# Query scores to a second bank, their casts four steps later, and one batch assigned three steps later

## The chip, the cores and the metric

The kernel runs on one core of one Trainium2 chip. The metric is the device time of one execution in microseconds (us), the median of several runs. In the profile of the kernel before, TensorE runs 4539 matrix multiplications, VectorE and ScalarE 561 and 502 instructions, mostly element by element, GpSimd 301, mostly copies and starts of transfers. Of the 272 transfers that it lists, SyncE starts 190, GpSimd 80 and ScalarE 2. The kernel puts the matrix results into PSUM, in rings of banks (`PS_BUFS` below). In profile lines PE is TensorE, PEld its weight loads, DVE VectorE, ACT ScalarE, POOL GpSimd and SPq the transfer queue of SyncE.

## The reference, cut to what matters

```python
# attention, batch 4, 8 heads, 768 positions, head size 64, 16 clusters
q_assign = argmax(q_n @ c_n)              # nearest centroid of every query
k_assign = argmax(k_n @ c_n)              # and of every key
scores = where(q_assign == k_assign, scale * q @ k.T, -1e9)
attn_out = softmax(scores) @ v
# mixture of 4 experts on the attention's output
for e in range(4):
    out += p[:, e:e+1] * (relu(x @ w1[e]) @ w2[e])
```

## The kernel before: the parts that the change touches

The kernel weaves three streams into one TensorE program: the attention in "steps" (24 for each unit of 256 query rows), the experts of earlier units, and the assignment of the next batch's keys and queries to clusters. The assignment of a batch is a schedule of small jobs.

```python
PS_BUFS = {"s": 2, "av": 1, "av2": 1, "mo": 3, "misc": 1}      # the rings of PSUM banks
...
def casts(self):                       # VectorE: transposed rows to bf16, for the attention
    ...
def scores_split(self, bank_tag):      # rows against the centroids, then two copies of the halves
    sc = bank(bank_tag)
    for x in range(HG):
        ...
        nc.tensor.matmul(sc[32 * x:32 * x + 32, :QW], lhs, rhs, start=True, stop=True)
    ...
    for s in range(2):
        dve(self.sch[:, s * QW:(s + 1) * QW], src[:, s::2])
...
def assigns(b):
    xs = ...                           # keys, queries of heads 0-3, then of heads 4-7
    for y, x in enumerate(xs):
        z = y % 2                      # 0: keys, 1: queries
        ...                            # (batch 1 in another way)
        t = 8 * y
        for j in range(HG):
            put(t + j, lambda x=x, j=j: x.split(j))         # GpSimd
            put(t + 2 + j, lambda x=x, j=j: x.cross(j))     # transposing transfer
            put(t + 9 + j, lambda x=x, j=j: x.merge(j))     # GpSimd
        put(t + 15, x.casts)                                # VectorE
        at = 16 * (y // 2) + 24
        put(at, lambda x=x: x.scores_split("mo"))           # both of a pair at once
        ...
# experts, on 256 rows: four banks of "mo" for the hidden rows, two for the output
for f in range(0, NF, per):
    ph = bank("mo")
    ...                                # 4 matmuls per 128 hidden columns (L728), Relu on ScalarE
for m, r in enumerate(rs):
    po = bank("mo")[:, c]
    ...                                # 8 matmuls (L747)
    nc.vector.scalar_tensor_tensor(oacc[:, c], po, pap, oacc[:, c], op0=ALU.mult, op1=ALU.add)  # L756
...
gens.append(Paced(late_queries(), 5, S1 - 6, S1 + 4))       # loads batch 1, among other things
for b in range(1, B):
    gens.append(Paced(assigns(b), XSTEPS[b], PER_B * (b - 1) if b > 1 else S1 + 4,
                      PER_B * b - 2))
```

A "pair" below is the scores of keys and queries of four heads, eight small matmuls each as the profile counts them. Batches 2 and 3 have two pairs each: 2a, 2b, 3a and 3b.

The softmax here doesn't subtract the row's maximum and nothing guards it: scores larger than these inputs give would overflow.

## Time and profile before

| | before |
|---|---|
| time of the first three runs | 482.76 us (482.57 to 483.82) |
| span of the profiled run | 480.9 us |
| TensorE busy, share of the last chain | 97%, 85% |
| granted TensorE clock | 1.0 throughout |

TensorE is the bound, so the time can be read as TensorE's work plus TensorE's stalls. Two views show the stalls: the list of its waits, and the distance in time between equal pieces of its work. The prediction shows both.

### The profile page before, as it was taken

What the parts mean: (1) busy time and instruction counts of PE and PEld (TensorE: products, weight loads), DVE (VectorE), ACT (ScalarE), POOL (GpSimd) and SP (SyncE); (2) the same over time, 40 slices, a digit from 0 to 9 for tenths busy, and PEclk for the clock granted to TensorE, in tenths of its full rate; (3) what the DMA queues carried; (4) which work ended last, traced back from release to release, by engine and by line L of the source; (5) the groups of instructions that cost most, each with busy time, mean ns of one, the idle gap of its engine ahead of it and who ended that gap; (6) DMA issues with size and microseconds to landing.
All of it is one profiled execution on the core that took longest, in us unless ns stands there. A gap on an engine that the chain in (4) does not pass through costs nothing.

```text
span 480.9 us, 11389 instructions
## 1 busy us (share of the span) xinstructions
PE 467.7 (97%) x4539; PEld 332.6 (69%) x4539; DVE 226.7 (47%) x561; ACT 277.4 (58%) x502; POOL 186.2 (39%) x301
## 2 busy tenths in 40 slices
PE   8998999999999989999999999999999999999997
PEld 4776777677775657767766776777666666766675
DVE  5864664222324562422234444431877867765112
ACT  5755656555564546656655665566566585574341
POOL 5937479273343667180145834000313222221000
PEclk9999999999999999999999999999999999999999
DMA  8999953824564743614565573312000100100101
GB/s 281 254 211 347 237 106 54 152 57 127 92 131 111 159 102 81 143 34 51 140 140 110 119 135 115 87 35 75 27 29 13 50 14 7 34 30 10 46 2 44
DMA packets 74557, 48.01 MB, mean 100 GB/s; under 512 B 50248, under 2 KB 69256, under 8 KB 74504
## 3 DMA queue, kind: packets, MB, share of 16 engines
q1 hardware_dynamic: 65256, 37.96, 31.8%
q0 software_dynamic: 8576, 9.25, 10.8%
q8 instruction: 35, 0.57, 0.5%
q10 hardware_dynamic: 672, 0.08, 0.1%
q14 instruction: 18, 0.15, 0.1%
HBM read 37.31 MB, written 6.30 MB: 91 GB/s over the span
## 4 chain that ended last, share of the span: by engine, by line
PE 85%; DMA 5%; DVE 3%; SPq 3%; POOL 2%; issue 1%; ACT 0%; POOLq 0%; DVEq 0%; ACTq 0%
PE ps_mo L728 32%; PE ps_mo L747 31%; PE ps_s L638 8%; PE ps_av L665 7%; DMA raw<-in_k_dram 4%; SPq L368 1%; PE ps_s L548 1%; DMA sct<-scs 1%; SPq L336 1%; PE ps_misc L242 1%; POOL t L377 1%; PE ps_mo L400 1%; PE ps_mo L242 1%; PE ps_misc L548 1%; DVE oacc L756 1%
## 5 line engine op out<-in xcount | busy, mean ns | idle before, releaser
L644 ACT ACTIVATE at<-ps_s 128x512 bf16<-128x512 f32 x252 | 147.9, 595 | 125.7 <-PE ps_s L638 110.5
L728 PE MATMUL ps_mo<-xT,w1b 128*128 128x256 bf16 (+1 forms) x1664 | 195.7, 264 | 0.0
L747 PE MATMUL ps_mo<-w2b,hT 128*128 128x512 bf16 (+1 forms) x776 | 189.9, 377 | 2.8 <-DVE oacc L756 2.8
L728 PEld LDWEIGHTS <-w1b 128*128 128x128 bf16 x1664 | 146.3, 98 | 24.1 <-issue 0.6
L734 ACT ACTIVATE hT<-ps_mo 128x512 bf16<-128x512 f32 x192 | 114.7, 598 | 60.7 <-PE ps_mo L728 57.6
L756 DVE SCALAR_TENSOR_TENSOR oacc<-ps_mo,psb,oacc 128x512 f32<-128x512 f32 (+1 forms) x73 | 54.2, 742 | 125.5 <-PE ps_mo L747 125.3
L747 PEld LDWEIGHTS <-hT 128*128 128x128 bf16 x776 | 67.2, 98 | 61.4 <-issue 6.6
L638 PE MATMUL ps_s<-qf,kf 80*128 80x256 bf16 (+1 forms) x456 | 82.8, 267 | 0.7 <-DVE t L252 0.4
L665 PEld LDWEIGHTS <-at 128*128 128x128 bf16 x1152 | 69.9, 97 | 15.3 <-issue 1.7
L665 PE MATMUL ps_av<-vx,at 128*128 128x65 bf16 x1152 | 80.3, 193 | 0.0
L651 POOL TENSOR_TENSOR at<-at,same 128x512 bf16<-128x512 bf16 x24 | 28.2, 1176 | 97.7 <-ACT at L644 82.2
L638 PEld LDWEIGHTS <-kf 80*128 80x128 bf16 x456 | 42.4, 98 | 20.7 <-issue 1.6
L565 DVE TENSOR_SCALAR same<-qf,late 128x256 bf16<-128x256 bf16 x144 | 39.1, 324 | 0.0
L377 POOL COPY t<-t 128x768 uint16<-128x768 uint16 x32 | 35.6, 1119 | 0.3 <-DMA t<-h 0.3
L651 DVE TENSOR_TENSOR at<-at,same 128x512 bf16<-128x512 bf16 x48 | 21.6, 451 | 25.9 <-ACT at L644 25.8
L358 POOL COPY h<-raw 128x768 uint16<-128x768 uint16 x16 | 13.0, 826 | 37.2 <-DMA raw<-in_q_dram 31.0
L754 DVE TENSOR_SCALAR oacc<-ps_mo,psb 128x512 f32<-128x512 f32 x18 | 13.5, 750 | 28.5 <-PE ps_mo L747 28.5
L361 POOL COPY h<-raw 128x768 uint16<-128x768 uint16 x16 | 13.0, 825 | 33.0 <-DMA raw<-in_q_dram 19.5
L336 POOL DMA_DIRECT2D kf<-oht x32 | 16.4, 526 | 22.9 <-DMA oht<-oh 14.2
L416 POOL COPY st<-sct 128x384 uint16<-128x384 uint16 x16 | 9.9, 662 | 37.5 <-DMA sct<-scs 37.2
L672 DVE RECIPROCAL zr<-ps_av 128x4 f32<-128x4 f32 (+1 forms) x50 | 8.9, 178 | 30.1 <-PE ps_av L665 30.0
L674 DVE TENSOR_TENSOR xn<-ps_av,zr 128x256 bf16<-128x256 f32 (+1 forms) x50 | 20.7, 414 | 1.7
(127 smaller groups left out, 284.8 us busy)
## 6 DMA issues: line engine op xcount, KB each, us to landing
raw<-in_v_dram SPq DMA_DIRECT2D x8, 768.0 KB, 5.6
out_dram<-oacc SPq DMA_DIRECT2D x23, 256.0 KB, 2.0
raw<-in_k_dram SPq DMA_DIRECT2D x7, 768.0 KB, 6.6
raw<-in_q_dram SPq DMA_DIRECT2D x6, 768.0 KB, 4.9
w1b<-in_moe_w_dram POOLq DMA_DIRECT2D x4, 1024.0 KB, 11.8
w2b<-in_moe_w_dram POOLq DMA_DIRECT2D x4, 1024.0 KB, 17.1
qf<-nos SPq DMA_DIRECT2D x2, 768.0 KB, 4.0
xT<-xn SPq DMA_TRANSPOSE x72, 2.4
```

The costliest lines, as they stand in the source:

```text
L336: (nc.gpsimd if self.b or self.i0 and self.g else nc.sync).dma_start(out=self.rows(slice(D, D + CL), j, r), in_=self.oht[p0:p0 + CL, :self.w])
L377: pool(self.all[:, y * w:(y + 1) * w].bitcast(U16)[:, z::2], self.t16[:, (2 * z + y) * w:(2 * z + y + 1) * w])
L565: nc.vector.tensor_scalar(same[:, x * 256:(x + 1) * 256], clusters(b)[:, g, w, k // 2, k % 2, :], key_nos[b % 2][:, g, 8 * i + 4 * (k // 2 ...
L638: nc.tensor.matmul(sp[:, x * n:(x + 1) * n], KF[b % 2][:K, h, r, i * 128:(i + 1) * 128], QF[b % 2][:K, h, rs[0]:rs[-1] + 1, w * 128:(w + 1 ...
L644: nc.scalar.activation(at, sp, ACT.Exp, scale=scale)
L651: (nc.gpsimd if n4 in POOL_STEPS else nc.vector).tensor_tensor(at, at, same_cluster(b, w, cur), op=ALU.mult)
L665: nc.tensor.matmul(av[:, h % 2, m, :], at[:, c0:c0 + 128], VX[b % 2][:, h, 2 * i + r, :], start=(first and x == 0 and m == 0), stop=(last ...
L674: nc.vector.tensor_tensor(xn[:, :nr].rearrange("p i j d -> p j i d"), av[:, :, :, :D], zr.broadcast_to([128, 2, nr, D]), op=ALU.mult)
L728: nc.tensor.matmul(ph[:, x * n:(x + 1) * n], W1[e][:, i, (f + x) * 128:(f + x + 1) * 128], xT[:, i, :], start=(i == 0), stop=(i == ND - 1))
L734: nc.scalar.activation(ht, ph, ACT.Relu)
L747: nc.tensor.matmul(po, hT[f // per][:, c0:c0 + 128], W2[e][:, f, c], start=(f == 0), stop=(f == NF - 1))
L756: nc.vector.scalar_tensor_tensor(oacc[:, c], po, pap, oacc[:, c], op0=ALU.mult, op1=ALU.add)
```

## The change

It is meant to remove stalls of TensorE: those at the pairs by taking the query scores out of the ring "mo" and the casts out of VectorE's way, and one at the start of batch 1 by letting its keys land first.

```diff
-                put(t + 15, x.casts)
+                put(t + 15 + 4 * z, x.casts)
...
-            put(at, lambda x=x: x.scores_split("mo"))
+            put(at, lambda x=x, t=("mo", "misc")[z]: x.scores_split(t))
...
-        gens.append(Paced(assigns(b), XSTEPS[b], PER_B * (b - 1) if b > 1 else S1 + 4,
-                          PER_B * b - 2))
+        gens.append(Paced(assigns(b), XSTEPS[b], PER_B * (b - 1) if b > 1 else S1 + 7,
+                          PER_B * b - (2 if b > 1 else -2)))
```

## The prediction

> **What bounds the kernel now.** I read the page's busy shares first, then TensorE's waits, then the chain of work that ended last, then the order in time of TensorE and VectorE around each wait.
>
> ```profile
> span 480.9 us, 11389 instructions
> PE 467.7 (97%) x4539; PEld 332.6 (69%) x4539; DVE 226.7 (47%) x561; ACT 277.4 (58%) x502; POOL 186.2 (39%) x301
> PE 85%; DMA 5%; DVE 3%; SPq 3%; POOL 2%; issue 1%; ACT 0%; POOLq 0%; DVEq 0%; ACTq 0%
> ```
>
> TensorE is busy for 97% of the span and carries 85% of the last chain. The change neither adds nor removes a matmul, so it can only win back time in which TensorE stands still: at most 480.9 − 467.7 = 13.2 us in all, and only what belongs to the three places that the change touches. TensorE's own waits (total us, times, longest) are:
>
> ```profile
> PE ps_mo L747 <- DVE oacc L756: 2.8, 2, 2.0
> PE ps_misc L242 <- DMA raw<-in_k_dram: 2.0, 2, 1.6
> ...
> PE ps_mo L400 <- DVE oacc L756: 1.0, 1, 1.0
> PE ps_misc L242 <- DVE t L252: 0.5, 2, 0.3
> ```
>
> L400 is the scores of keys and queries against the centroids in batches 2 and 3; L756 is the VectorE pass that empties an expert's output bank; L242 transposes the raw keys and queries of batch 1. The first and third lines are waits for a bank of the three-bank ring "mo". The second pair of scores in batch 2 shows how such a wait arises (start us, duration, then the idle time before and its releaser); first TensorE, then VectorE:
>
> ```profile
> 175.12 0.59 PE L747 MATMUL ps_mo<-w2b,hT 128*128 128x512 bf16 x2
> 175.65 1.50 PE L400 MATMUL ps_mo<-t,bdc 128*32 128x384 f32 x16
> 179.13 1.02 PE L747 MATMUL ps_mo<-w2b,hT 128*128 128x512 bf16 x4 [1.98 <-DVE oacc L756]
> ```
>
> ```profile
> 176.07 2.22 DVE L387 CAST qf<-t 64x1536 bf16<-64x1536 f32 x2
> 178.32 0.75 DVE L756 SCALAR_TENSOR_TENSOR oacc<-ps_mo,psb,oacc 128x512 f32<-128x512 f32 x1
> 178.99 1.94 DVE L404 COPY scs<-ps_mo 128x384 uint16<-128x384 uint16 x4
> ```
>
> The first expert output is complete at 175.12 + 0.59 = 175.7 in one bank. The two scores take the other two banks of "mo". The next output needs the first bank again, but VectorE empties it only at 178.3, because the casts of the queries stand before it in VectorE's program. TensorE waits from 177.15 to 179.13.
>
> [...] L756 was ready at 175.7 and ran at 178.32, right after the casts ended at 176.07 + 2.22 = 178.29. [...]
>
> **The change part by part.**
>
> *Scores and casts, batches 2 and 3.* An expert on 256 rows repeats its instructions, so the distance between equal pieces of the last chain gives the cost of a pair with its stall inside:
>
> ```profile
> 255.42 1.31 PE ps_mo L728 x12
> ...
> 265.96 1.31 PE ps_mo L728 x12
> ...
> 274.97 1.31 PE ps_mo L728 x12
> ...
> 283.99 1.31 PE ps_mo L728 x12
> ...
> 295.45 1.31 PE ps_mo L728 x12
> ```
>
> A plain period is 283.99 − 274.97 = 9.02 us. The first pair of batch 3 (no wait recorded) takes 265.96 − 255.42 = 10.54, so 1.52 is the scores' own work, as the 1.50 of the 16 matmuls confirms. The second pair takes 11.46, a stall of 0.92. The same subtraction in batch 2, between the 12-matmul pieces in TensorE's order of time, gives 152.60 − 140.84 = 11.76, a stall of 1.22, for the first pair. For the second it gives, from the chain, 183.35 − 161.77 − 9.01 = 12.57, a stall of 2.03. The sum is 1.22 + 2.03 + 0.92 = 4.17 us; the recorded waits alone make 1.00 + 1.98 + 0.87 = 3.85.
>
> In the changed kernel the query scores go to "misc", which batches 2 and 3 leave idle until the last batch's attention begins. A pair then takes one bank of "mo", so the next expert output finds the third bank, which ScalarE emptied long before. Independently, the queries' casts (two of 0.96 us in batch 2, one of about 1.0 in batch 3) move four of this stage's steps later. By the order of VectorE's instructions they now come after the L756 pass, the four score copies and the next L756 pass. In the first pair of batch 2 this removes a second delay too: VectorE stood 3.63 us at its head of queue for GpSimd's last merge before those casts. The casts still cost the same 1.9 us, but lie where TensorE needs no bank for at least two outputs (2 × 8 matmuls × 0.216 = 3.5 us). I count all 4.17 as won.
>
> *Batch 1 three steps later.* The first transpose of the keys waits for their load:
>
> ```profile
> 39.23 0.28 PE L665 MATMUL ps_av<-vx,at 128*128 128x65 bf16 x4
> 41.13 0.52 PE L242 MATMUL ps_misc<-ident,raw 128*128 128x128 f32 x3 [1.62 <-DMA raw<-in_k_dram]
> ```
>
> The load is issued at 33.25 and lands 7.75 us later, at 41.0; TensorE arrives at about 39.5. In the changed instruction order three groups of two expert matmuls, two attention scores and four value matmuls come before this transpose. From 41.49 to 42.26 such a group takes 0.77 us, so TensorE arrives at 39.5 + 3 × 0.77 = 41.8, some 0.8 us after the load. That wait (1.62) should vanish. The transposes of the keys then come farther apart, because expert and attention work lies between them, so most of the 0.34 and 0.18 us waits for the single "misc" bank should go too. I count 1.62 + 0.3 = 1.9 us. All matmuls remain.
>
> *Sum.* 4.17 + 1.9 = 6.1. I subtract 0.1 for new small waits: queries' transposes of the second head group now follow each other closely in "mo". 482.76 − 6.0 = 476.8, which I round down to 476.6, since restarts after a stall cost a few hundredths each that go as well.
>
> **The rivals.** First, *the delay only moves the wait*: batch 1's queries, keys and weights come later, and something behind them becomes late. I counted along the new order: the attention of the last four heads of the first unit pulls from 49.4 forward to about 46.2 us, and needs query rows that GpSimd sends from 38.6 on. They take 5.1 us from issue to landing, so the first two are there by 44.7, a margin of 1.5 us. The raw queries land about 12 us after their issue at 33.88, at 46.1, and are needed at 47.7. The scores of the first half of batch 1 come at about 52.6 instead of 52.2, so GpSimd's later work (last expert's weights, sends, casts of the values, finished at 101.6 before) shifts by about a microsecond, against more than 4 us of slack. If one margin fails, 1 to 2 us come back: 478 to 479.
>
> Second, *the casts stall another bank*: at their new place they delay a later L756 or the normalisation that frees an attention bank. VectorE is only 20 to 40% busy there outside the pairs, and the keys' casts, already at such places (at 160.48, 2.32 us), made no TensorE wait. If it happened, some 2 us would come back: about 479.
>
> Third, *a slower engine sets the pace* behind the bank wait, GpSimd's merges: in the first pair of batch 2 the last merge ends at 145.3, and the query scores need it at about 147.1. The load that feeds it follows VectorE's and the transposing queue's work, which moves forward with TensorE. I hold this unlikely; it would bring back under 1 us.
>
> **How the range and the chances follow.** With every stall gone and restarts too, 482.76 − 4.2 − 2.1 − 0.5 = 476.0, and run-to-run spread (1.25 us over the three runs before) widens that downwards to 475.0. With one rival true the time is 478 to 479, so I take 479.2 as the upper end. Faster by over 2% would need 473.1, a gain of 9.7 us, more than all the stalls that the change touches; slower by over 2% would need some 16 us of new waits. I give these 0.02 and 0.01.
>
> **What would show it right or wrong.** Right: TensorE's list of waits loses both L756 lines and the 1.6 us raw-key wait; all four pairs of scores take about 10.5 us per period; L756 runs at once after its matmuls, with the queries' casts after the score copies. Wrong: a raw load or query rows before L242 or L638 between 41 and 50 us, an L747 or L728 that waits for VectorE after the moved casts, or L400 waiting for GpSimd.

That VectorE keeps its program's order at this place is what the trace shows: L756 at 178.32, 0.03 us after the casts, 2.6 us after its matmuls.

Four figures of the prediction with what they rest on. The 0.216 is the time of an L747 matmul in the last chain (2.16 us for the ten at 102.59). The "few hundredths" of a restart compare with the period's stall less the recorded wait, 0.05 us at 2b and at 3b, and 0.22 at 2a; the 0.5 us for restarts in the range is measured nowhere. The 12 us of the raw queries are an estimate: the profile before gives no landing for that load, and the keys' load issued next, at 34.43, took 11.2 us. (In the changed kernel the two loads of raw queries issued at 33.82 and 35.82 took 11.8 us in the median.)

## The result, and the profile after

The changed kernel takes 476.11 us (475.66 to 476.71, four runs) and the kernel before 482.66 (482.14 to 483.82, four runs). The ratio is 0.9862, with a 95% interval from 0.9841 to 0.9883. Ratios here are the mean time of one kernel's fast runs over that of the other's of the same rounds, so not quite the ratio of the medians.

The page of the changed kernel, its span, busy times and the shares of its last chain:

```profile
span 474.2 us, 11333 instructions
PE 464.6 (98%) x4488; PEld 333.1 (70%) x4539; DVE 228.7 (48%) x561; ACT 277.2 (58%) x502; POOL 187.8 (40%) x301
PE 95%; DVE 2%; DMA 1%; issue 1%; ACT 1%; SPq 0%; ACTq 0%
```

The span fell by 6.7 us. TensorE's share of the last chain rose from 85% to 95%, which says that less is left in the chain but TensorE's own work. (Its busy time must not be compared: 51 of 4539 matmul records are missing in this trace.) TensorE's waits in the changed kernel, the first two and the last but one of its list:

```profile
PE ps_s L87 <- DVE blank L80: 1.2, 1, 1.2
PE ps_s L638 <- DVE t L252: 0.4, 1, 0.4
...
PE ps_mo L681 <- DVE xn L674: 0.2, 1, 0.2
```

The 1.2 us are at the very start and were there before. The waits for L756, for the raw keys of batch 1 and for the bank "misc" in batch 1 are gone. The place of pair 2b, first TensorE in order of time, then VectorE:

```profile
171.21 0.59 PE L747 MATMUL ps_mo<-w2b,hT 128*128 128x512 bf16 x2
171.74 0.85 PE L400 MATMUL ps_mo<-t,bdc 128*32 128x384 f32 x8
172.41 1.05 PE L400 MATMUL ps_misc<-t,bdc 128*32 128x384 f32 x8
173.39 1.04 PE L747 MATMUL ps_mo<-w2b,hT 128*128 128x512 bf16 x4
```

```profile
172.60 0.73 DVE L756 SCALAR_TENSOR_TENSOR oacc<-ps_mo,psb,oacc 128x512 f32<-128x512 f32 x1
173.25 1.01 DVE L404 COPY scs<-ps_mo 128x384 uint16<-128x384 uint16 x2
174.18 1.01 DVE L404 COPY scs<-ps_misc 128x384 uint16<-128x384 uint16 x2
...
178.23 1.91 DVE L387 CAST qf<-t 64x1536 bf16<-64x1536 f32 x2
```

The next expert output starts 0.98 us after the query scores began, without a wait for VectorE; the casts have moved behind everything that TensorE needed. The first transpose of batch 1:

```profile
41.48 0.28 PE L665 MATMUL ps_av<-vx,at 128*128 128x65 bf16 x4
41.60 0.52 PE L242 MATMUL ps_misc<-ident,raw 128*128 128x128 f32 x3
```

It follows the value matmuls by 0.12 us, where the kernel before stood still.

The period around pair 2b, from the last chain of the changed kernel (start us, us, what):

```profile
166.87 1.31 PE ps_mo L728 x12
...
177.63 1.31 PE ps_mo L728 x12
```

**Where the 6.7 us came from.** I split the span at pieces of work that are the same in both traces. "Stretch 1" runs from the eight 256-column score matmuls of batch 0 (L267, at 33.95 before, 33.88 after) to the first group of 24 hidden-row matmuls (89.23 and 86.53). For the pairs I take the period between 12-matmul pieces of L728 and subtract 9.01 us (plain period) and 1.54 us (the pair's own work), so 10.55 is a pair without a stall.

| | before | after | won |
|---|---|---|---|
| before stretch 1 | 33.95 | 33.88 | 0.07 |
| stretch 1 (batch 1) | 55.28 | 52.65 | 2.63 |
| period with pair 2a | 11.76 | 10.55 | 1.21 |
| period with pair 2b | 12.58 | 10.76 | 1.82 |
| period with pair 3a | 10.55 | 10.54 | 0.0 |
| period with pair 3b | 11.47 | 10.54 | 0.93 |

The sum is 6.66 us of the 6.7.

### The profile page after: what moved, and what is told of

The parts are those of the page before. It is cut to its first block, busy times and chain, and to the rows that moved or that the text cites. A ratio compares the mean times of both kernels' runs of the same rounds, so it can differ in the third digit from the quotient of the medians.

```text
span 474.2 us, 11333 instructions
## 1 busy us (share of the span) xinstructions
PE 464.6 (98%) x4488; PEld 333.1 (70%) x4539; DVE 228.7 (48%) x561; ACT 277.2 (58%) x502; POOL 187.8 (40%) x301
## 4 chain that ended last, share of the span: by engine, by line
PE 95%; DVE 2%; DMA 1%; issue 1%; ACT 1%; SPq 0%; ACTq 0%
PE ps_mo L728 35%; PE ps_mo L747 34%; PE ps_s L638 10%; PE ps_av L665 8%; PE ps_s L548 1%; DMA raw<-in_q_dram 1%; PE ps_misc L242 1%; PE ps_mo L242 1%; PE ps_misc L548 1%; PE ps_mo L400 1%; PE ps_misc L267 1%; PE ps_misc L400 1%; PE ps_mo L267 0%; DVE oh L287 0%; DVE mx L284 0%
## 5 line engine op out<-in xcount | busy, mean ns | idle before, releaser
L728 PE MATMUL ps_mo<-xT,w1b 128*128 128x256 bf16 (+1 forms) x1664 | 195.8, 264 | 0.0
L747 PE MATMUL ps_mo<-w2b,hT 128*128 128x512 bf16 (+1 forms) x725 | 186.2, 377 | 2.3
L728 PEld LDWEIGHTS <-w1b 128*128 128x128 bf16 x1664 | 146.3, 98 | 25.0 <-issue 1.2
L756 DVE SCALAR_TENSOR_TENSOR oacc<-ps_mo,psb,oacc 128x512 f32<-128x512 f32 (+1 forms) x73 | 54.1, 742 | 125.2 <-PE ps_mo L747 120.7
L747 PEld LDWEIGHTS <-hT 128*128 128x128 bf16 x776 | 67.0, 98 | 57.5 <-issue 3.1
L377 POOL COPY t<-t 128x768 uint16<-128x768 uint16 x32 | 36.2, 1141 | 0.0
L336 POOL DMA_DIRECT2D kf<-oht x32 | 15.4, 495 | 24.3 <-DMA oht<-oh 15.1
L336 POOL DMA_DIRECT2D qf<-oht x40 | 20.3, 516 | 4.0 <-DVE oht L313 3.9
```

Of the source, the lines that this page charges most:

```text
L336: (nc.gpsimd if self.b or self.i0 and self.g else nc.sync).dma_start(out=self.rows(slice(D, D + CL), j, r), in_=self.oht[p0:p0 + CL, :self.w])
L377: pool(self.all[:, y * w:(y + 1) * w].bitcast(U16)[:, z::2], self.t16[:, (2 * z + y) * w:(2 * z + y + 1) * w])
L728: nc.tensor.matmul(ph[:, x * n:(x + 1) * n], W1[e][:, i, (f + x) * 128:(f + x + 1) * 128], xT[:, i, :], start=(i == 0), stop=(i == ND - 1))
L747: nc.tensor.matmul(po, hT[f // per][:, c0:c0 + 128], W2[e][:, f, c], start=(f == 0), stop=(f == NF - 1))
```

## The experiments

All twelve kernels gave right results. Kernels of one call ran on one chip and share their runs of the kernel before. The stalls are from the profiled run, by the subtraction just explained.

| kernel | call | median, range (us) | before, same call | ratio, 95% interval | stalls 2a, 2b, 3a, 3b | stretch 1 |
|---|---|---|---|---|---|---|
| before | | 482.66, 482.14-483.82 | | | 1.21, 2.03, 0, 0.92 | 55.28 |
| after | | 476.11, 475.66-476.71 | 482.66 | 0.9862, 0.9841-0.9883 | 0, 0.21, 0, 0 | 52.65 |
| e1_ring | 1 | 478.26, 477.98-478.36 | 484.12 | 0.9878, 0.9836-0.9919 | 0, 0.03, 0, 0 | 54.67 |
| e2_casts | 1 | 478.34, 478.16-479.28 | 484.12 | 0.9885, 0.9849-0.9921 | 0, 0.61, 0, 0.50 | 54.29 |
| e3_late | 1 | 479.85, 478.42-480.12 | 484.12 | 0.9906, 0.9868-0.9944 | 1.25, 0.14, 0, 1.28 | 52.64 |
| e4_ring_casts | 1 | 478.46, 478.09-478.79 | 484.12 | 0.9883, 0.9848-0.9918 | 0, 0, 0, 0 | 55.15 |
| e5_early | 2 | 482.33, 481.84-483.68 | 482.98 | 0.9980, 0.9953-1.0008 | 0.81, 2.49, 0.51, 0.95 | 53.49 |
| e6_late_one | 2 | 482.69, 480.84-484.51 | 482.98 | 0.9971, 0.9937-1.0004 | 0.91, 2.23, 0, 2.69 | 55.33 |
| e7_one_ring | 2 | 482.55, 481.90-485.21 | 482.98 | 0.9991, 0.9954-1.0027 | 1.44, 1.43, 1.44, 1.83 | 52.64 |
| e8_before_double | 2 | 493.91, 493.43-494.84 | 482.98 | 1.0218, 1.0192-1.0244 | 4.46, 5.74, 1.27, 3.84 | 55.18 |
| e9_after_double | 3 | 476.89, 476.23-477.90 | 482.82 | 0.9874, 0.9840-0.9909 | 0, 0.90, 0, 0 | 52.66 |
| e10_after_early | 3 | 476.18, 475.49-476.95 | 482.82 | 0.9860, 0.9831-0.9888 | 0, 0.46, 0, 0 | 52.64 |
| e11_pair_later | 4 | 476.11, 475.59-476.39 | 482.46 | 0.9862, 0.9840-0.9883 | 0, 0, 0, 0 | 52.64 |
| e12_ring_late | 4 | 476.07, 475.91-477.08 | 482.46 | 0.9869, 0.9849-0.9889 | 0, 0.17, 0, 0 | 52.64 |

In call 1 the kernel before itself ranged from 482.35 to 486.08. The granted clock shows why. Of the 28 runs of the kernel before, the ten with a mean clock of 0.993 or 0.996 took 483.87 to 486.08 us, and the eighteen with 0.999 or 1.0 took 481.99 to 483.53. Four of the seven in call 1 are of the first kind, so the ratios of that call flatter all four kernels alike; the other three have a median of 482.57, close to the 482.66 of the result, with which the four kernels are compared below. A trace in which the clock falls is that of e8. No run of e1 to e4, of e9 to e12 or of the changed kernel has a clock below 0.999.

### e1_ring: the second bank alone

```diff
-            put(at, lambda x=x: x.scores_split("mo"))
+            put(at, lambda x=x, t=("mo", "misc")[z]: x.scores_split(t))
```

> The kernel before with only the query scores of batches 2 and 3 sent to the bank misc; casts and batch 1 as before. Theory A (bank and cast order are two remedies for one wait, each enough by itself): with the third bank of mo free, the next expert output no longer needs the bank that waits behind VectorE's casts, so the three stalls of 1.22, 2.03 and 0.92 us vanish except for the wait for GpSimd's last merge in the second pair of batch 2 (0.2 us in the changed kernel): a gain of about 4.0 us, 478.7 us, and periods with a pair of 10.55, 10.75, 10.54, 10.55. Rival B (each part owns its share of the 4.2): about 2 us of gain, 480.6, with stalls left in the pairs. Rival C (only the cast order matters): no gain, 482.7.

Measured: 478.26 us, 4.4 below the 482.66 of before, and no stall in the pairs above 0.03 us. Theory A holds, B and C fall. Stretch 1 is a little shorter than before (54.67): this run came to it 0.25 us later, and its first transpose of the keys started 0.35 us earlier (40.78 against 41.13), so that the wait for the keys was 0.60 us shorter (1.02 against 1.62). The change of e1 does not touch that place.

### e2_casts: the casts alone

```diff
-                put(t + 15, x.casts)
+                put(t + 15 + 4 * z, x.casts)
```

> The kernel before with only the queries' casts of batches 2 and 3 four steps later; all scores still in mo. Theory A: VectorE now empties the first expert output at once, so the bank comes free in time although both scores sit in mo. In batch 2 both stalls nearly vanish; in the second pair of batch 3 the emptying still stands behind the numbering of the clusters on VectorE, and moves forward by only 0.67 us, so some 0.2 to 0.4 us of the 0.92 stay. Gain about 3.7 us, 479.0. Rival B: about 2 us, 480.6. Rival C turned round (only the bank matters): no gain, 482.7.

Measured: 478.34 us, 4.3 below the 482.66. The stalls of 2a and 3a are nil, 0.61 is left in 2b and 0.50 in 3b. In 3b VectorE reaches the emptying only after the work that stands before it (0.45 us recorded). In 2b no wait of a matmul is recorded. The weight loads of L400 waited for GpSimd's merges (L377; 0.9 us in two waits over the whole run), and the sixteen matmuls of this pair took 2.12 us in place of 1.50. Here too theory A holds: either remedy takes away most of the same wait. The size was near; a stall of 0.61 in 2b was more than I had allowed. The profiled run was the slowest of the four (479.28).

### e3_late: batch 1 alone

```diff
-PER_B * (b - 1) if b > 1 else S1 + 4,   PER_B * b - 2
+PER_B * (b - 1) if b > 1 else S1 + 7,   PER_B * b - (2 if b > 1 else -2)
```

> The kernel before with only batch 1 three steps later. From the two traces the three waits of batch 1 cost 1.78, 0.51 and 0.35 us counted from issue to issue (1.62, 0.34 and 0.18 as recorded idle time). If these waits are all of it, the gain is 2.64 us, 480.0, and all four pairs keep their stalls of before (periods 11.76, 12.57, 10.54, 11.46). Rival: part of the 2.7 us belongs to the interplay with the other parts, then less than 2 us here.

Measured: 479.85 us, 2.8 below the 482.66, against 2.64 expected. Stretch 1 is 52.64, exactly that of the whole change. The pairs' stalls did not stay as before: 3b is longer, and 2b nearly vanished in the profiled run (0.14), which was the fastest of the four (478.42). There VectorE began the queries' casts at 171.47, 1.47 us before the scores of 2b; in the kernel before it began them 0.42 us after. These stalls vary from run to run as long as their cause is there.

### e4_ring_casts: both remedies of the pairs, no delay of batch 1

The first two hunks of the change.

> The bank and the casts changed, batch 1 as before. Theory A: the two remedies overlap, so the gain is that of the better one and not the sum: about 4.0 us, 478.7, with periods of about 10.55 (10.75 for the second pair of batch 2). Together with the 2.64 us of batch 1 alone this makes the 6.6 us of the whole change. Rival B: the sum of the gains of bank alone and casts alone, each about 2 us.

Measured: 478.46 us and four pairs at 10.54 to 10.55. Bank alone gave 478.26, casts alone 478.34, both 478.46: the gains do not add. This is shown by three kernels on one chip.

### e5_early: another cure for the first wait of batch 1

```diff
-        19: lambda: (qc.onehot(), qc.keep(), qc.send_all()),
+        19: lambda: (qc.onehot(), qc.keep(), load_raw(), qc.send_all()),
...
     def late_queries():
-        load_raw()
```

> The kernel before, batch 1 not delayed, but the load of its first raw keys is issued ahead of the eight sends of query rows that stood before it in the same queue (they took from 28.22 to 33.2 us). If the late load is the cause of the 1.78 us wait, the load now lands some 5 us earlier, the wait goes without any delay of batch 1, and the two waits for misc (0.51 and 0.35) stay: a gain of about 1.8 us, 480.9. The query rows behind it come 0.5 us later. Rival (TensorE was held up at this place by something else that the delay cured, such as the bank misc): no gain, 482.7.

The transfer queue of this kernel (start us, duration):

```profile
22.87 0.52 SPq L130 DMA_DIRECT2D raw<-in_k_dram  x1
28.67 7.34 SPq L336 DMA_DIRECT2D qf<-oht  x8
```

The load left at 22.87 in place of 33.25, and stretch 1 shrank by 55.28 - 53.49 = 1.79 us, the expected size: the late load is the cause, and the wait for it is worth 1.78. But the time fell by 0.65 us only, with an interval that includes none, so the time itself does not show the gain. Two of the four runs (483.68 and 482.67) had a mean clock of 0.996; the two others took 481.84 and 481.99. Two more things took it back in the profiled run: the stretch began 0.64 us later (34.59), and the pairs' stalls sum to 4.76 us in place of 4.16. The later start need not come from the change: e2, which is unchanged up to there, started its stretch at 34.61, and the starts of all profiles lie between 33.83 and 34.61. Why the stalls of the pairs were longer in this run is not settled.

### e6_late_one: a delay of one step

```diff
-PER_B * (b - 1) if b > 1 else S1 + 4,
+PER_B * (b - 1) if b > 1 else S1 + 5,
```

> The kernel before with batch 1 begun one step later in place of three, its end as before. One group of expert and attention work (0.77 us) now comes before the first transpose, so the wait for the raw keys should be about 1.78 - 0.77 = 1.0 us from issue to issue, 0.85 as recorded; the waits for misc may stay (0.5 to 0.9). Gain 0.8 to 1.2 us, 481.6. Rival (any delay is enough, because the gain comes from a better mix of work): the full 2.6 us, 480.0.

TensorE's waits in this kernel, from 36 to 44 us and from 52 to 60 us:

```profile
PE ps_misc L242 <- DMA raw<-in_k_dram: 0.9, 1, 0.9
```

```profile
PE ps_mo L681 <- DVE xn L674: 1.0, 1, 1.0
```

The wait for the keys shrank to 0.9 as expected, but stretch 1 is 55.33, no shorter. A new wait took its place: the normalised attention rows (L674) now stand on VectorE behind a burst of batch 1's work, and TensorE waits 1.04 us for them. The time is 482.69 against an expected 481.6. The profiled run was the slowest of four that went from 480.84 to 484.51; its stalls at the pairs sum to 5.83 us against 4.16 before. My expectation had only counted the waits that were there. So three steps are not merely a longer delay; they also put batch 1's work where it meets nothing.

### e7_one_ring: both scores of a pair in "misc"

```diff
-            put(at, lambda x=x, t=("mo", "misc")[z]: x.scores_split(t))
+            put(at, lambda x=x: x.scores_split("misc"))
```

> The changed kernel, but both scores of a pair go to the single bank misc and none to mo. If what counts is that no two users of one bank follow each other closely, the query scores now wait until VectorE has copied the key scores out of misc: from the changed kernel's trace that is 145.55 - 144.28 = 1.3 us in the first pair of batch 2, 174.26 - 172.41 = 1.85 in the second, and about 1.3 and 1.7 in batch 3, together about 6 us: 482. If only the relief of mo counts, nothing is lost: 476.1.

The head of TensorE's waits:

```profile
PE ps_misc L400 <- DVE scs L404: 5.3, 4, 1.6
```

Measured: 482.55 us, and stalls of 1.44, 1.43, 1.44 and 1.83 that sum to 6.15. What counts is that each score finds a bank that is free: one bank for both is not enough. Two rings are not needed for that, as e2 shows, where both scores stayed in the three banks of "mo" and 2a and 3a had no stall.

### e8_before_double: the queries' casts twice, in the kernel before

```diff
                 put(t + 15, x.casts)
+                if z:
+                    put(t + 15, x.casts)
```

> The kernel before with the queries' casts of batches 2 and 3 done twice in a row, the same values to the same place. If VectorE's casts ahead of the emptying are what TensorE waits for, each microsecond added there appears in the time: 1.9 us more in each pair of batch 2, about 1 us in the second pair of batch 3, nearly nothing in the first pair of batch 3, so 487.5. If the stalls only stem from the two scores in mo, the casts lie beside other work: 482.7.

Measured: 493.91 us, 10.9 us over before, more than twice the 4.8 that I expected. TensorE at pair 2b:

```profile
184.21 1.03 PE L749 MATMUL ps_mo<-w2b,hT 128*128 128x512 bf16 x4 [4.03 <-DVE oacc L758]
```

Line numbers are two higher here. The recorded waits grew by about what the second casts cost: 1.00 to 2.59 at 2a, 1.98 to 4.03 at 2b, none to 1.06 at 3a, 0.87 to 2.12 at 3b, together 5.95 us. So VectorE's casts are indeed what TensorE waits for.

The other five microseconds are the second half of the lesson. In this trace the granted clock fell to 0.50 at 150.96, 185.09 and 301.14, that is 1.4, 0.9 and 0.6 us after the waits at 2a, 2b and 3b had ended, each time for about 3.4 us. (Four matmuls of L749 at 151.24 held TensorE for 1.69 us until the next piece, in place of 0.86.) The stretches around the first fall (start and end, length, then busy us and instructions of PE, PEld, DVE, ACT, POOL, the granted clock, the DMA share and GB/s):

```profile
149.00:150.00 1.00, 0.46 (x8) 0.19 (x8) 1.00 (x3) 0.00 (x0) 0.00 (x0) 1.00 0.26 54
150.00:151.00 1.00, 1.00 (x12) 0.41 (x5) 0.87 (x3) 0.00 (x0) 0.00 (x0) 0.98 1.00 366
151.00:152.00 1.00, 1.00 (x8) 0.51 (x6) 0.47 (x2) 0.60 (x1) 0.00 (x0) 0.50 0.90 336
152.00:153.00 1.00, 1.00 (x4) 0.36 (x3) 0.00 (x0) 0.00 (x0) 0.14 (x1) 0.50 0.02 8
153.00:154.00 1.00, 1.00 (x7) 0.67 (x5) 0.75 (x1) 0.00 (x0) 1.00 (x2) 0.50 0.00 0
154.00:155.00 1.00, 1.00 (x12) 0.87 (x11) 0.00 (x0) 0.49 (x1) 1.00 (x2) 0.81 0.03 8
155.00:157.00 2.00, 2.00 (x24) 1.81 (x22) 0.61 (x2) 1.75 (x4) 2.00 (x3) 1.00 0.00 0
```

I estimate the cost from such stretches, as what the clock lacks of 1.00 times the length: here 0.02 + 3 × 0.50 + 0.19 = 1.71 us, and in the same way 1.72 and 1.71 at the other two, together 5.1 us.

At pair 2b of e5 a recorded wait of 2.19 us (until 178.04) did not lower the clock:

```profile
176.00:180.00 4.00, 1.96 (x14) 1.09 (x14) 3.79 (x7) 0.60 (x1) 4.00 (x8) 1.00 0.70 176
180.00:182.00 2.00, 2.00 (x23) 1.71 (x21) 0.75 (x1) 0.98 (x2) 1.99 (x5) 1.00 1.22 238
```

Nor did the 1.98 us of the kernel before at the same pair (1.00 in every stretch from 174 to 183 us), while the 2.12 us at 3b of e8 were followed by a fall. So the length of a wait alone does not tell whether the clock falls after it; what does is not shown by these runs.

### e9_after_double: the queries' casts twice, in the changed kernel

The same doubling after the change's own line.

> The changed kernel with the queries' casts done twice at their new place. If that place has the slack claimed for it (two expert outputs before a bank is needed again), the added 1.9 us in each pair of batch 2 and about 1 us in batch 3 cost nothing: 476.1, within 0.5. If the new place only just fits, up to 5 us appear.

Measured: 476.89 us, 0.8 over the changed kernel and a little outside the expected 0.5. Pairs 2a, 3a and 3b have no stall; 2b has 0.90, which is a wait of the query scores for GpSimd's merge (1.0 us at the weight loads of L400), not for a bank. The place of the casts has the slack claimed for it where banks are concerned; that GpSimd was later in this run may come from the casts, but is not shown to.

### e10_after_early: the changed kernel with the early load too

The two hunks of e5_early on top of the change.

> The changed kernel with the load of batch 1's raw keys also issued ahead of the query sends. In the changed kernel TensorE reaches the first transpose some 0.6 us after the load has landed, so an earlier load should win nothing: 476.1, within 0.5. If other work waited for that load or the query rows behind it are now late, the time moves by up to 1 us either way.

Measured: 476.18 us and a stretch 1 of 52.64. Once the wait is gone, an earlier load wins nothing.

### e11_pair_later: the second pairs one step later

```diff
-                at = 16 * (y // 2) + 24
+                at = 17 * (y // 2) + 24
```

> The changed kernel with the second pair of scores of batches 2 and 3 one step later. In the changed kernel the second pair of batch 2 still lost 0.21 us (0.46 in a sister run) against the plain period and its work, because the query scores wait for GpSimd's last merge. If that is the cause, one step (1.5 us) more removes it: the period with this pair becomes 10.55, and the time falls by 0.2 to 0.5 us, to about 475.8, too little for the timed runs to show surely. If the leftover has another cause, the period stays at 10.7 to 11.0.

Measured: the period with 2b is 19.56 - 9.01 = 10.55, and the weight loads of L400 no longer wait for GpSimd: its last merge ended at 172.94, the scores began at 174.06. So the leftover of 0.21 us fits GpSimd's merge, and a later pair avoids it. This is one profile, and the leftover varies without the step too (none in e4, 0.46 in e10). The time of 476.11 us does not tell it from the changed kernel; the gain, if there is one, is below what five rounds resolve. No version beat the changed kernel.

### e12_ring_late: the whole change without the casts' move

The second and third hunks of the change.

> The kernel before with the second bank and the later batch 1, but the queries' casts left where they were. If bank and cast order are two remedies for the same wait, the casts' move is not needed: 476.1, the same as the whole change, with pairs at 10.5 to 10.8. If the casts' move gives something of its own, the time is up to 2 us longer.

Measured: 476.07 us. The casts' move can be left out at no cost that these runs show.

## Why the prediction was right, point by point

**What bounds the kernel: right.** The gain came from stalls of TensorE alone: the pieces of the table add up to 6.66 of 6.7 us.

**The stalls of the pairs, 4.17 us: right in mechanism, 0.2 us too much.** 3.96 us were won. Pair 2b kept 0.21 us, most likely a wait for GpSimd's last merge (in e11, with the pair a step later, neither is there). This is the third rival, which I had looked for in pair 2a, where there was no sign of it. The four shares measured by the period (1.22, 2.03, 0, 0.92) were each won as worked out, 2b apart.

**Two remedies, one wait.** The prediction treated bank and casts as one step and said that the casts' order helps "independently". The experiments say more: in the profiles the bank alone takes away 4.13 and the casts alone 3.05 of the 4.16 us, both together 4.16 (e1, e2, e4), and in the whole change the casts' move is idle (e12). The waits are removed when either the bank is not needed or the emptying is not delayed.

**Batch 1, 1.9 us: right in mechanism, too small.** The term measured 2.63 us in the trace and 2.64 in e3. I took the recorded idle times, 1.62 and "most of" 0.34 and 0.18. But what a stall costs is the time from the issue of the last matmul before it to the issue of the first after it, less the usual pitch. The value matmuls at 39.23 have a pitch of 0.12 us and a recorded length of 0.28, so at this pitch the next would have started at 39.35; it started at 41.13, a loss of 1.78. For the other two waits the same count gives 0.51 and 0.35, and 1.78 + 0.51 + 0.35 = 2.64. The profile's idle begins at the recorded end of the last matmul, and at that group 0.28 − 0.12 = 0.16 us lie between the usual issue of the next and this end. I had made this correction for the pairs by using periods, and not here; the 0.5 us set aside for restarts covered it in the range only, and the "few hundredths each" that the prediction gave a restart were 0.16 to 0.17 here. No run here tells whether the recorded ends are late or the matmuls really overlap.

**The arrival at the first transpose: right.** Predicted 41.8 us after three groups of 0.77; measured 41.60. The load, issued at 33.19, had landed 7.6 us later, at 40.8.

**The first rival, a wait that only moves: not in the changed kernel, but real.** No margin that I had counted failed. With one step in place of three it happened (e6): 0.74 us less waiting for keys (0.88 in place of 1.62), 1.04 us more waiting for VectorE.

**The second rival, casts that stall another bank: did not happen.** Even twice the casts stalled no bank (e9). But the prediction had their cost wrong for the new place: it said "the same 1.9 us", and they took 3.29 us in place of 1.92 at 2a and 1.58 in place of 0.96 at 3a (1.91 and 0.95 at 2b and 3b, no longer than before). It cost nothing: the changed kernel's list of TensorE's waits has none for L756. At 2a the moved casts ran beside copies of GpSimd, which took longer too, 1.77 and 1.58 us in place of 1.04 and 0.82:

```profile
149.69 3.29 DVE L387 CAST qf<-t 64x1536 bf16<-64x1536 f32 x2
```

```profile
150.41 1.77 POOL L377 COPY t<-t 128x768 uint16<-128x768 uint16 x1
152.09 1.58 POOL L361 COPY h<-raw 128x768 uint16<-128x768 uint16 x1
```

In the kernel before, GpSimd's last copy there had ended at 145.29 when the casts began at 145.32. At 3a of the changed kernel a copy of GpSimd beside the cast took 1.77 us as well. What makes both slower is not isolated by a run.

**The chances and the range.** 476.11 lies within 475.0 to 479.2 and 0.5 us under the predicted 476.6; the missing 0.7 us of batch 1 less the 0.2 us of pair 2b explain it.

**What stays open.** The kernel before varied more (482.0 to 486.1 over all calls) than those without its stalls (475.5 to 477.1 over after, e10, e11 and e12). The profiles show that its stalls differ between runs (2b: 2.03, 0.14 in e3, 2.49 in e5). Its longest runs had a lowered clock (ten of 28; one fall to 0.50 for 3.4 us, as in e8, in 482 us gives a mean of 0.996). That a wait at a pair brought it about would fit e8, but no profile of such a run was taken. Part of what the ratios show is thus that such runs are gone; the 6.7 us between the two profiles are without it, since in neither did the clock fall while TensorE worked (before: 1.00 throughout; after: 1.00 up to 473 us, and its last matmuls ended at 470.9).

## What to carry to other kernels

When TensorE waits for a bank, look at what stands before the emptying in the other engine's program: moving that, or taking one user out of the ring, cured the same wait here (478.34 and 478.26 us, against 482.66), and doing both gave no more (478.46). Count a stall from issue to issue or by the period of repeated work, since the recorded idle time left out 0.16 to 0.17 us of each of three short waits here (1.62, 0.34 and 0.18 against 1.78, 0.51 and 0.35). And before you delay a job to let its data land, look for what its work will then meet: one step in place of three only traded one wait for another here (e6). And a duration taken from a trace for an instruction that is to be moved may not hold at the new place: the casts of 2a took 3.29 us there in place of 1.92.
